# Attention with 32 heads beside a long convolution: one step of sixteen in four late stacks has its exponentials computed on VectorE, and the output projection is reordered

## The chip, the core and the metric

The kernel runs on one core of a Trainium2 chip. The core has five engines that run their own instruction streams and meet only through semaphores: TensorE (PE, matrix products, with its weight loads listed as PEld), VectorE (DVE), ScalarE (ACT, activation functions such as the exponential), GpSimd (POOL) and SyncE (SP, which here only issues DMAs). TensorE writes into PSUM, a small memory of eight banks; DVE and ACT read it from there. The metric is the device time of one execution in microseconds. The time before is 1044.47 us, the median of three runs (1041.78, 1044.47, 1046.85).

## What is computed

Two independent results stand side by side in the output, 2048 rows of 512 + 512 columns, all in float32.

```python
# A: attention, 32 heads of 16, one key and one value head for all of them
q = (x @ wq).reshape(B, S, H, Dh).transpose(0, 2, 1, 3)
k, v = x @ wk, x @ wv
p = softmax(einsum("bhqd,bkd->bhqk", q, k) * Dh ** -0.5)
a = einsum("bhqk,bkd->bhqd", p, v).transpose(0, 2, 1, 3).reshape(B, S, H * Dh) @ wo
...
# B: short causal convolution (4 taps) of k, times v, long causal convolution by FFT, gated by q
kv = shift_conv(k, shift_k) * v
y = irfft(rfft(pad(kv)) * rfft(pad(ssm_k))) + kv * ssm_D
b = q * y
```

Part A has 32 x 2048 x 2048 exponentials. They are the largest single piece of work in the kernel.

## The kernel before

**Attention.** The 32 heads times 2048 queries are cut into 32 *stacks* (`NQ`), each of four heads times 512 queries. A stack walks over the 2048 keys in 16 steps of 128 (`NKT`), and each step has two tiles of 128 keys by 2 x 512 scores. For each tile `scores` (the matmuls of L909) writes the scores into one of two PSUM buffers, `exp` (L921) has ACT turn them into probabilities in SBUF with one instruction of 128 x 1024, and `pv` (L941) multiplies both tiles of a step with V, extended by ones so that the row sums come along, into two PSUM banks that hold the sums of the whole stack. So there are 32 x 32 = 1024 exponential instructions. When a stack's last step is multiplied, DVE evicts the sums (L952, L953) and SP sends them to DRAM (L956). The last stack, 31, is cut in another way: two halves of 256 queries, each with 16 tiles.

**The frame.** `attend` is the main loop. One turn x is a *slot*: it emits the scores and the exponential of tile x + 2, then the V products that `plan` puts into this slot, and then hands the rest of the slot to `_Fill`. The order of every engine's instructions is thus written out when the program is built; nothing moves at run time, and an instruction that waits holds up all that follows it on its engine. The slot number within a stack is what is called "slot 14 of stack 26" below.

**The fill.** All other work runs as Python generators, called threads, which `_Fill.turn` asks in a fixed order, unless `hurry` puts one of them first. A thread asks for PE work as a number of units (216 ns each), with a charge for the DVE work that follows, or for DVE work alone (0 units and a charge in ns), or waits a number of steps of two slots (`WAIT`). PE units are given only as far as the account of the slot allows (916 ns a slot, 220 for scores, 430 for each half of a V product). DVE work is given while the credit is positive; it grows by 850 ns a slot, up to 1700. A thread whose next request is marked `CONT` holds the filler's PSUM pair, and no other thread gets PE work until it is done; after that two slots pass (`GAP`). The pool `pf` has two pairs of banks: one holds the sums of the running stack, the other is for the fill. Most fill matmuls go through `halves`: a first half, a tiny memset on DVE (`look`, L244) that marks its end, and a second half that waits for it. Their matmuls carry line L232.

**The threads**, in their order before: `wo_heads` brings the sums of two stacks (a *group* G of eight heads) back from DRAM, takes the reciprocal of the row sums (L1004, L1005), sends them through DRAM once more and forms normalised head outputs in 16-bit parts (L1016); `conv_pe` loads for the convolution and does its transforms on PE, in the order short transform of block 0, long transforms, output products of block 0 (`backward`, evicted by L450), short transform of block 1 (evicted by L272), output products of block 1; `conv_short` forms the short products on DVE; `rest_of_q` makes the other query chunks; `wo_part` does the output projection for chunks of 512 rows, each of four groups (L1058), then groups 12 and 13 (L1068), 14 (L1082), and the rest of the last group (L1095, after `over`, L1106 to L1112); `conv_dve` does the 16-point transforms and the products in the frequency domain on DVE (lines L152 to L203, L417); `spill` moves transposed inputs out to DRAM and back. Only four normalised groups fit at once, so group G waits until group G - 4 has been projected.

**The end.** After the last slot, `last` finishes the last V products, normalises the last quarter and adds its projection to the partial sums of the last chunk.

Of the kernel before, what the change touches and what calls it, by code (L numbers as in the profile page):

```python
# [8 lines left out]
F32 = mybir.dt.float32  # L9
F32R = mybir.dt.float32r  # L10
BF16 = mybir.dt.bfloat16
F16 = mybir.dt.float16
I32 = mybir.dt.int32
# [47 lines left out]
GAP = 2  # L61

# [36 lines left out]
class _Emit:  # L99
# [614 lines left out]
    def prologue(self):  # L714
        nc = self.nc
        zero = self.w.tile([P, 512], F16, tag="gn", bufs=3, name="zero")
        nc.vector.memset(zero, 0.0)
        self.load()
# [18 lines left out]
        nc.scalar.mul(self.wq[0][:, 0], self.wqf[0], WS)  # L737
        nc.vector.scalar_tensor_tensor(self.wq[0][:, 1], self.wqf[0], WS, self.wq[0][:, 0], ALU.mult, ALU.subtract)
# [11 lines left out]
        for g in range(1, 4):  # L750
            self.parts(nc.gpsimd, self.wq[g][:, 0], self.wq[g][:, 1], self.wqf[g], WS)
# [49 lines left out]
    def hurry(self):  # L801

        c, g = self.qn
        if c < 4 and self.step >= 2 * NKT * (4 * c + g) - LEAD:
            return 3
        return 4 if any(self.step >= x and ("wo", 4 * c) not in self.seen for c, x in enumerate(WO_AT)) else None
# [86 lines left out]
    def place(self, u):  # L893

        n = u // (2 * NKT)
        if n == NQ - 1:
            h = u // NKT % 2
            return n, u % NKT, slice(0, 2), slice(256 * h, 256 * h + 256)
        return n, u // 2 % NKT, u % 2, slice(0, 512)

    def scores(self, u):


        n, k, a, cols = self.place(u)
        s = self.ps.tile([P, 2, 512], F32, tag="s", name=self.nm("s"))
        for e in range(2):
            rows = slice(64 * e, 64 * e + KR)
            for j in range(0, P, 32):
                self.nc.tensor.matmul(  # L909
                    s[j : j + 32, e, :],  # L910
                    self.kst[rows, k * P + j : k * P + j + 32],
                    self.st[n][rows, a, cols],
                    start=True,
                    stop=True,
                )
        return s

    def exp(self, u, s):

        self.pt[u] = self.w.tile([P, 2, 512], F32, tag="p", bufs=PB, name=self.nm("p"))  # L920
        self.nc.scalar.activation(self.pt[u], s, AF.Exp, scale=DH**-0.5 / SC / SC)  # L921

    def pv(self, x, part):

        nc = self.nc
        n, k, _, cols = self.place(x)
# [4 lines left out]
        if k == 0:  # L931
            b = self.pair()
            self.acc = [b[:, 0, :], b[:, 1, :]]
        for e in range(2):
            rows = slice(64 * e, 64 * e + 64)
            for j in range(4):
                if wide:
# [3 lines left out]
                nc.tensor.matmul(  # L941
                    self.acc[e][32 * j : 32 * j + 32, m], self.vx[rows, k, :], y, start=k == 0, stop=k == NKT - 1
                )
        if k < NKT - 1:
            return
# [12 lines left out]
    def plan(self):  # L958


        plan = {}
        last = 2 * NKT * (NQ - 1)
        for x in range(0, last, 2):
            k = x // 2 % NKT
            if k == 1:
                for part, late in enumerate((1, 3)):
                    plan.setdefault(x + 1 + late, []).append((x, part))
            else:
                plan.setdefault(x + 1 + 2 * (k == 0), []).append((x, None))
        for x in range(last, 2 * NQ * NKT):  # L970
            plan.setdefault(x + {0: 2, 1: 1, 2: 1, 3: 1}.get(x % NKT, 0), []).append((x, None))
        cost = {i: sum(2 if x < last and part is None else 1 for x, part in v) for i, v in plan.items()}
        return plan, cost

    def attend(self, fill):
        self.od = self.dr.tile([NQ, P, 512], F32, name="od")
        tiles = 2 * NQ * NKT
        plan, cost = self.plan()
        for x in range(tiles - 2):
            t = x + 2  # L980
            if t % 32 == (22 if t < 32 else 12) and t // 32 + 1 < NQ:
                self.stack(t // 32 + 1)
            self.exp(t, self.scores(t))
            self.step, self.slot = x // 2, x
            for y in plan.get(x, []):
                self.pv(*y)
            fill.turn(x, cost.get(x, 0), cost.get(x + 1, 0))
# [3 lines left out]
    def heads(self, G):  # L991
# [10 lines left out]
        yield WAIT, 3  # L1002
# [10 lines left out]
        yield WAIT, 2  # L1013
# [35 lines left out]
    def wo_part(self):  # L1049
        nc, w, I = self.nc, self.w, self.I  # L1050
        xr = self.out.rearrange("b (c p i) d -> (b c) p i d", c=4, p=P, i=4)
        for c in range(3):
            yield from self.after(("oc", 4 * c + 3))
# [7 lines left out]
            self.seen.update(("wo", G) for G in range(4 * c, 4 * c + 4))  # L1061

# [8 lines left out]
        for q in range(2):  # L1071
            t = w.tile([P, D], F32, tag="xt", bufs=2, name=self.nm("wl"))
# [41 lines left out]
    def last(self, fill):  # L1114
# [5 lines left out]
        self.pv(2 * NQ * NKT - 2, None)  # L1120
# [4 lines left out]
        self.pv(2 * NQ * NKT - 1, None)  # L1125
# [14 lines left out]
class _Fill:  # L1140
# [29 lines left out]
    def give(self, t, n, i):  # L1170
        self.go(t, n or None)
        if n:
            self.holder = t if t[1] is not None and len(t[1]) > 2 and t[1][2] == CONT else None
            if self.holder is None:
                self.free = i + GAP

    def turn(self, i, pvs, more):
# [5 lines left out]
        while more:  # L1183
            more = False
            first = self.hurry()
            for t in sorted(self.threads, key=lambda t: t is not self.threads[first or 0]):
# [13 lines left out]
                self.give(t, n, i)  # L1200
# [131 lines left out]
def body(ctx, tc, I, out, parts="ab"):  # L1332
    fpool = ctx.enter_context(tc.tile_pool(name="fl", bufs=1))
    ok = fpool.tile([1, 1], I32, name="ok")
    with ExitStack() as st:
# [4 lines left out]
        threads = [em.wo_heads(), em.conv_pe(), em.conv_short(), em.rest_of_q(), em.wo_part(), em.conv_dve(), em.spill()]  # L1340
# [26 lines left out]
```

## Time and profile before

| | |
|---|---|
| median of three runs | 1044.47 us (1041.78 to 1046.85) |
| the profiled execution | 1042.55 us, its span 1040.5 us |
| mean granted TensorE clock | 0.979 of full speed |
| exponentials | 1024, 947.6 us of ACT's time |
| first and last exponential start | 32.55 us, 1021.2 us |
| from the last exponential's end to the end | about 18 us |
| DVE busy | 686.1 us of the span |

A row of the page gives busy time, share and number of instructions of each engine. The chain of work that ended last is followed back from the last instruction, at each step to what released it. Rows of instruction groups have the form: line, engine, operation, out<-in with shapes, count, then busy time, mean duration in ns, and the idle time of the engine before them with what ended it. Rows of a timeline have start, duration, engine, line, operation and count. "f" is the filler's PSUM pair (and the stack's sums), "s" a score tile, "p" its exponentials, "sp" a spectrum of the convolution, "ao" the evicted sums of a stack, "st" the queries of a stack, "xT" the transposed input.

### The profile page before, as it was taken

Reading aid. Unit: us, or ns where it says so; the run is one execution under the profiler, and the core shown is the slowest. Engines: PE = TensorE matmul, PEld = TensorE weight load, DVE = VectorE, ACT = ScalarE, POOL = GpSimd, SP = SyncE. Lnnn points to the kernel's source line nnn. Section 1 sums busy time; section 2 is a strip of 40 time slices with the busy share of each in tenths; the row PEclk is TensorE's granted clock in tenths of the full one; section 3 lists DMA queues with packets and bytes.
Section 4 is the critical chain, followed back from the end, with each engine's and each line's share of the span. In section 5 each row is a group of like instructions: output and inputs, shape, how many; then the busy total and the mean of one; then the engine's idle time right before and its main releaser. Section 6 shows DMA issues by size and latency. Waiting matters only on the chain.

```text
span 1040.5 us, 51057 instructions
## 1 busy us (share of the span) xinstructions
PE 956.9 (92%) x23391; PEld 466.4 (45%) x23391; DVE 686.1 (66%) x1023; ACT 960.1 (92%) x1040; POOL 171.2 (16%) x305
## 2 busy tenths in 40 slices
PE   7999999899988999999999999999988899999885
PEld 4344444344544444444444544544433344554352
DVE  4537866799626888989859843686898993221133
ACT  4599998899997999999999989999999999999983
POOL 2541304200031000010231423321000000330000
PEclk9699999999998999999999999999999999999998
DMA  6271524413252121211332324321111112330101
GB/s 228 84 213 50 163 86 106 105 48 89 63 103 72 44 70 39 75 45 53 87 108 78 106 87 125 109 75 51 48 49 47 36 41 63 105 124 20 52 3 44
DMA packets 69315, 83.11 MB, mean 80 GB/s; under 512 B 20800, under 2 KB 58278, under 8 KB 69094
## 3 DMA queue, kind: packets, MB, share of 16 engines
q1 hardware_dynamic: 47142, 43.51, 13.5%
q0 software_dynamic: 20320, 35.46, 12.2%
q8 instruction: 185, 3.03, 1.2%
q10 hardware_dynamic: 1632, 0.81, 0.3%
q14 instruction: 36, 0.29, 0.1%
HBM read 54.66 MB, written 25.03 MB: 77 GB/s over the span
## 4 chain that ended last, share of the span: by engine, by line
ACT 46%; PE 33%; issue 9%; DVE 8%; DMA 3%; SPq 0%; ACTq 0%; DVEq 0%
ACT p L921 46%; PE f L941 15%; PE s L909 9%; PE f L232 7%; DVE sp L152 2%; DMA rd<-rl 1%; DMA r<-rd 1%; DVE ao L952 1%; DVE ao L953 1%; DMA xb<-in_A_x 1%; PE f L600 1%; DVE sp L272 1%; DVE a L387 1%; DVE t L378 0%; DMA qd<-qp 0%
## 5 line engine op out<-in xcount | busy, mean ns | idle before, releaser
L921 ACT ACTIVATE p<-s 128x1024 f32<-128x1024 f32 x1024 | 947.6, 1067 | 42.3 <-PE s L909 39.5
L941 PE MATMUL f<-p,vx 64*32 64x512 f32 (+1 forms) x8944 | 561.4, 560 | 2.5 <-DVE sp L272 1.1
L909 PE MATMUL s<-st,kst 49*32 49x512 f16 x8192 | 431.3, 385 | 37.2 <-ACT p L921 33.9
L909 PEld LDWEIGHTS <-kst 49*32 49x32 f16 x8192 | 199.0, 90 | 404.3 <-issue 362.5
L941 PEld LDWEIGHTS f<-p,vx 64*32 64x32 f32 x8944 | 179.6, 107 | 37.2 <-issue 10.4
L152 DVE TENSOR_TENSOR sp<-sp 128x1024 f32<-128x1024 f32 x96 | 111.4, 1214 | 3.1 <-issue 1.9
L272 DVE COPY sp<-f 128x512 f32<-128x512 f32 x64 | 41.1, 684 | 51.2 <-PE f L232 50.9
L277 POOL DMA_DIRECT2D ff<-in_ff x64 | 34.3, 545 | 199.8 <-PE s L909 192.3
L152 DVE TENSOR_TENSOR sp<-sp,sp 128x1024 f32<-128x1024 f32 x48 | 56.0, 1216 | 5.2 <-issue 3.6
L232 PE MATMUL f<-wo,o 64*32 64x512 f16 x1440 | 56.6, 375 | 3.0 <-DVE look L244 3.0
L452 POOL DMA_DIRECT2D out<-r x32 | 17.5, 550 | 247.6 <-DVE r L450 247.6
L244 DVE MEMSET look<- 128x4 f32 x67 | 4.2, 62 | 80.5 <-PE f L232 80.5
L232 PE MATMUL f<-xT,wq 64*32 64x512 f16 x1344 | 51.6, 376 | 5.1 <-DVE gm L712 2.6
L232 PE MATMUL f<-hT,ff 64*32 64x256 f32 x1024 | 42.8, 385 | 9.2 <-DVE look L244 8.5
L952 DVE COPY ao<-f 128x512 f32<-128x512 f32 (+1 forms) x33 | 22.3, 675 | 38.3 <-PE f L941 38.2
L232 PE MATMUL f<-a,ff 64*32 64x256 f32 x1024 | 42.0, 378 | 4.3 <-DVE look L244 3.4
L232 PE MATMUL f<-sp,fi 64*32 64x256 f32 x1024 | 41.0, 383 | 1.8 <-DVE look L244 1.8
L369 POOL DMA_DIRECT2D v<-in_B_v x32 | 17.0, 536 | 121.9 <-PE s L909 55.0
L378 DVE TENSOR_TENSOR t<-kk,tpb 128x512 f32<-128x512 f32 (+1 forms) x50 | 33.0, 663 | 3.1 <-issue 2.7
L387 DVE TENSOR_TENSOR a<-a,t 128x512 f32<-128x512 f32 x48 | 33.2, 691 | 2.6 <-DVE t L378 1.2
L450 DVE TENSOR_TENSOR r<-f,q 128x256 f32<-128x256 f32 x32 | 12.1, 419 | 32.0 <-PE f L232 32.0
L232 PEld LDWEIGHTS <-o 64*32 64x32 f16 x1440 | 22.8, 93 | 16.3 <-DVE look L244 3.6
(154 smaller groups left out, 681.6 us busy)
## 6 DMA issues: line engine op xcount, KB each, us to landing
ff<-in_ff POOLq DMA_DIRECT2D x64, 128.0 KB, 3.3
od<-ao SPq DMA_DIRECT2D x60, 128.0 KB
qd<-qp SPq DMA_DIRECT2D x48, 128.0 KB
st<-qd SPq DMA_DIRECT2D x62, 98.0 KB
kk<-in_B_k POOLq DMA_DIRECT2D x32, 128.0 KB, 3.9
v<-in_B_v POOLq DMA_DIRECT2D x32, 128.0 KB, 2.6
hin<-in_B_ssm_k POOLq DMA_DIRECT2D x32, 128.0 KB, 6.9
fi<-in_fi POOLq DMA_DIRECT2D x32, 128.0 KB, 3.5
```

The costliest lines, as they stand in the source:

```text
L152: v.tensor_tensor(part(out), part(a), part(b), op)
L232: y = self.nc.tensor.matmul(out[j : j + 32, cols], w[r, j : j + 32], x[r], start=half == m == 0, stop=half == 1 and m == k - 1,)
L272: self.nc.vector.tensor_copy(c[:, :, m + i, :], b[i].rearrange("p (q n) -> p q n", q=2))
L277: self.nc.gpsimd.dma_start(t[:, i], self.I[n][:, 2 * m2 + i])
L369: nc.gpsimd.dma_start(v[:, i], self.vr[:, 2 * m2 + i, cs])
L378: nc.vector.tensor_tensor(out[:, n], kk[:, x], tap(i, n.stop - n.start), ALU.mult)
L387: nc.vector.tensor_tensor(a, a, t, ALU.add)
L452: nc.gpsimd.dma_start(self.orr[:, 2 * m2 + i, D + blk * CB : D + (blk + 1) * CB], r[:, i])
L909: self.nc.tensor.matmul(s[j : j + 32, e, :], self.kst[rows, k * P + j : k * P + j + 32], self.st[n][rows, a, cols], start=True, stop=True,)
L921: self.nc.scalar.activation(self.pt[u], s, AF.Exp, scale=DH**-0.5 / SC / SC)
L941: nc.tensor.matmul(self.acc[e][32 * j : 32 * j + 32, m], self.vx[rows, k, :], y, start=k == 0, stop=k == NKT - 1)
L952: nc.vector.tensor_copy(a, self.acc[0][:, m])
```

## The change

In stacks 27, 28, 29 and 30 the last step, keys 1920 to 2047, is taken out of the main loop: `tiles` lists the tiles that remain, 30 instead of 32 in these stacks, and 1016 in all. A new thread `own`, first in the order, computes this step. It takes a pair of the filler's PSUM for the scores of each of the two tiles, from slot 14 of the stack before. On DVE it then adds a large constant that rounds the score to a whole number (the scores now come in units of ln 2, since the query weights are divided by it), subtracts again to get the fraction, builds the power of two by writing the rounded part as a 16-bit integer whose bits are read as a bfloat16 exponent, and evaluates a polynomial of the fraction by five fused multiply-add passes, the last of which multiplies by the power of two. The probabilities come out scaled by a constant, which a scaled copy of V (`vo`) takes back. From slot 8 of the stack, `attend` adds the product of this step in two parts.

```diff
+OWN_IN = (27, 28, 29, 30)
+OWN_AT, OWN_PV = 14, 8
...
-        self.nc.scalar.activation(self.pt[u], s, AF.Exp, scale=DH**-0.5 / SC / SC)
+        self.nc.scalar.activation(self.pt[u], s, AF.Exp, scale=LN2 * DH**-0.5 / SC / SC)
...
+    def own(self):
...
+        for n in OWN_IN:
+            while self.slot < 32 * n - 32 + OWN_AT or self.owed:
+                yield WAIT, 1
+            for a in range(2):
+                yield (1, 2400, CONT, 1, 4) if a else (1, 2400, NEW, 1)
+                b = self.pair()
+                self.keys(b, n, OWN, a, slice(0, 512))
+                v.tensor_scalar(self.po[:, a], b, MAGIC, None, ALU.add)
+                v.scalar_tensor_tensor(f[:, a], self.po[:, a], MAGIC, b, ALU.subtract, ALU.subtract)
+                if a == 0:
+                    yield WAIT, 1.5, CONT
+            for a in range(2):
+                g, y = self.po[:, a], f[:, a]
+                x = self.w.tile([P, 2, 512], I16, tag="s2", bufs=S2, name=self.nm("x"))
+                yield 0, 900
+                v.tensor_scalar(x, g, 2.0**-11, (127 - DOWN) * 128 - MAGIC * 2.0**-11, ALU.mult, ALU.add)
+                for i in range(4, -1, -1):
+                    yield 0, 1220
+                    v.scalar_tensor_tensor(g, g if i < 4 else y, c[i], y if i else x.bitcast(BF16), ALU.add, ALU.mult)
+            self.owed = [(-1 - n, part) for part in range(2)]
...
-            if t % 32 == (22 if t < 32 else 12) and t // 32 + 1 < NQ:
-                self.stack(t // 32 + 1)
+            n = self.at[t][0]
+            if t - self.base[n] == (6 if n else 22) and n + 1 < NQ:
+                self.stack(n + 1)
...
+            if self.owed and self.owed[0][0] == -1 - n:
+                part, in_stack = self.owed[0][1], x - self.base[n]
+                if in_stack >= 5 + part * (NKT - 1) if n == NQ - 1 else in_stack >= OWN_PV and not pvs:
+                    pvs = [self.owed.pop(0)] + pvs
```

The output projection changes its order: chunk 1 also waits until block 1's short transform is done, and chunk 2 is done in two pieces, groups 8 to 10 into a partial sum in SBUF, then group 11 on top of it. The pauses in the head work get shorter, and the two zero-padded weight tiles of the last group (`wl`) lie in another buffer, since `own` uses theirs (`xt`).

```diff
-        yield WAIT, 3
+        yield WAIT, 2
         yield 0, 400
         nc.vector.tensor_scalar(l, l, 1e-30, 1 / OS, ALU.max, ALU.mult)
...
-        yield WAIT, 2
+        yield WAIT, 1.5
...
-        for c in range(3):
-            yield from self.after(("oc", 4 * c + 3))
+        for c in range(2):
+            yield from self.after(("oc", 4 * c + 3), *[("cx", 1)] * c)
...
+        yield from self.after(("oc", 10), "q3")
+        wp = [w.tile([P, D], F32, tag="wq", bufs=4, name=self.nm("wp")) for _ in range(4)]
+        for i in (0, 2):
+            b = yield from self.wo_rows(i, range(8, 11), 1400)
+            for r in range(2):
+                nc.vector.tensor_scalar(wp[i + r], b[r], 1 / (OS * WS), None, ALU.mult)
+        self.seen.update(("wo", G) for G in range(8, 11))
+        yield from self.after(("oc", 11))
+        for i in (0, 2):
+            b = yield from self.wo_rows(i, [11], 1400)
+            for r in range(2):
+                t = self.s2("wp", (512,))
+                nc.vector.scalar_tensor_tensor(t, b[r], 1 / (OS * WS), wp[i + r], ALU.mult, ALU.add)
...
-            t = w.tile([P, D], F32, tag="xt", bufs=2, name=self.nm("wl"))
+            t = self.s2("wl", (512,))
...
-        threads = [em.wo_heads(), em.conv_pe(), em.conv_short(), em.rest_of_q(), em.wo_part(), em.conv_dve(), em.spill()]
+        threads = [em.own(), em.wo_heads(), em.conv_pe(), em.conv_short(), em.rest_of_q(), em.wo_part(), em.conv_dve(), em.spill()]
```

More of the change, by code (lines that the diff above doesn't have):

```diff
@@ L968, in plan @@
             else:
[L969 to L972, printed above, removed]
-        return plan, cost
+                plan.setdefault(x + 1 + 2 * (k == 0), []).append((x, None, x + 2 == self.base[n + 1]))
+        for x in range(last, len(self.at)):
+            k = self.at[x][1]
+            plan.setdefault(x + {0: 2, 1: 1, 2: 1, 3: 1}.get(k, 0), []).append((x, None, k == self.at[-1][1]))
@@ new lines, in plan @@
+        cost = {i: sum(2 if x[0] < last and x[1] is None else 1 for x in v) for i, v in plan.items()}
+        return plan, cost
+    def own(self):
+        nc, v = self.nc, self.nc.vector
+        c = [x / TWO[5] * (-(2.0**18)) ** (5 - i) for i, x in enumerate(TWO)]
+        self.vo = self.msk[:, 163:195]
+        done = [f"q{c}" for c in range(4)]
+        yield from self.after(*done)
+        yield 0, 100
+        v.tensor_scalar(self.vo, self.vx[:, OWN, :], -TWO[5] * 2.0 ** (DOWN - 90), None, ALU.mult)
+        room = [self.w.tile([P, 2, 4, 512], F16, tag="xt", bufs=2, name=self.nm("own")) for _ in range(2)]
+        self.po = room[0].rearrange("p i k n -> p (i k n)").bitcast(F32).rearrange("p (a e n) -> p a e n", a=2, e=2)
+        f = room[1].rearrange("p i k n -> p (i k n)").bitcast(F32).rearrange("p (a e n) -> p a e n", a=2, e=2)
+        for n in OWN_IN:
[18 more added lines that the diff above has]
+            self.owed = [(-1 - n, part) for part in range(2)]
+        self.seen.add("own")
```

84 lines of the change are left out of this document (53 added, 31 removed).

## The prediction, made before the changed kernel was run

> **What bounds the kernel now.** First the page: span, busy shares and the chain of work that ended last.
>
> ```profile
> span 1040.5 us, 51057 instructions
> PE 956.9 (92%) x23391; PEld 466.4 (45%) x23391; DVE 686.1 (66%) x1023; ACT 960.1 (92%) x1040; POOL 171.2 (16%) x305
> ACT 46%; PE 33%; issue 9%; DVE 8%; DMA 3%; SPq 0%; ACTq 0%; DVEq 0%
> ```
>
> ACT and PE are equally busy over the span, so the answer has to come from the stage that changes. Next, the timeline of ACT alone at the end (start, duration, line, operation, count; idle before it in brackets), then a table by stretches of one stack each, 26 to 30, and last stack 31 (length, then busy time of PE, weight loads, DVE, ACT, POOL; granted clock).
>
> ```profile
> 839.25 162.56 ACT L921 ACTIVATE p<-s 128x1024 f32<-128x1024 f32 x177
> 1004.45 1.02 ACT L921 ACTIVATE p<-s 128x1024 f32<-128x1024 f32 x1 [2.64 <-PE s L909]
> 840.98:870.30 29.32, 28.64 (x760) 13.88 (x752) 24.32 (x30) 29.32 (x33) 0.00 (x0) 1.00 0.12 37
> 870.30:899.63 29.33, 27.97 (x728) 14.15 (x720) 6.92 (x16) 29.33 (x33) 6.41 (x12) 1.00 0.35 110
> 899.63:928.96 29.33, 29.20 (x776) 15.17 (x768) 7.18 (x19) 29.33 (x33) 10.69 (x20) 1.00 0.41 128
> 928.96:958.29 29.33, 28.73 (x760) 14.13 (x752) 4.22 (x10) 29.33 (x33) 3.14 (x6) 1.00 0.12 38
> 958.29:987.62 29.33, 25.66 (x624) 11.70 (x616) 5.40 (x11) 29.33 (x33) 0.00 (x0) 1.00 0.17 47
> 987.62:1022.30 34.68, 31.14 (x984) 19.84 (x968) 11.28 (x28) 31.06 (x34) 0.00 (x0) 0.95 0.02 4
> 872.93 0.69 DVE L952 COPY ao<-f 128x512 f32<-128x512 f32 x1
> 902.32 0.69 DVE L952 COPY ao<-f 128x512 f32<-128x512 f32 x1 [0.43 <-PE f L941]
> ```
>
> From 839 to 1002 there is no idle moment between 177 exponentials: 162.56/177 = 0.918 us each. A stack is 32 of them, 29.3 us, and the eviction that closes a stack (L952) comes 902.32 - 872.93 = 29.39 us after the one before. ACT sets the pace in stacks 27 to 30, while DVE works only 4 to 7 of each 29.3 us there (24 of 29.3 in stack 26). So an exponential taken away in this stage is worth its full 0.918 us, as long as neither PE nor DVE takes over.
>
> **The change, part by part.** *Eight exponentials go.* Stacks 27 to 30 lose both tiles of step 15, two exponentials each: 8 x 0.918 = -7.3 us. Their score matmuls and their products with V stay on PE, moved into the fill between the steps. The rescaling of the query projection by 1/ln 2 alters constants of existing instructions and costs nothing.
>
> *What DVE gets.* Per tile: two passes out of PSUM (rounding, fraction), one to 16-bit integers, five fused passes for the polynomial. DVE's groups with shapes kept apart (busy, mean ns of one):
>
> ```profile
> L201 DVE TENSOR_SCALAR u<-sp 128x1024 f32<-128x1024 f32 x18 | 12.4, 689 | 0.4
> L575 DVE SCALAR_TENSOR_TENSOR xT<-f,xT 128x1024 f16<-128x1024 f32 x4 | 4.8, 1220 | 3.3 <-ACT xT L572 3.3
> L152 DVE TENSOR_TENSOR sp<-sp 128x1024 f32<-128x1024 f32 x96 | 111.4, 1214 | 3.1 <-issue 1.9 <-DVE sp L152 1.2
> L1058 DVE TENSOR_SCALAR wp<-f 128x512 f32<-128x512 f32 x12 | 7.7, 686 | 24.2 <-PE f L232 24.2
> ```
>
> A one-tensor pass from PSUM has a row only at half width, 0.69; full width lies between that and twice it, and I take 1.22, like the fused pass from PSUM. The integer pass is nearest to L201, 0.69 (at most 1.22). A fused pass in SBUF with two full tensors is nearest to L152, 1.22. One tile: 2 x 1.22 + 0.69 + 5 x 1.22 = 9.2 us; a stack 18.5, all four 74 us. The chain of stack n starts at slot 14 of stack n-1; it charges the filler 2 x 2400 + 2 x (900 + 5 x 1220) = 18800 ns, which at 850 ns per slot takes 22 slots, so it ends at slot 4 to 6 of stack n, before slot 8 where its product may enter. The idle DVE time of the stretches (29.3 - 7.2 = 22 us at the least) covers 18.5 us: 0 on the path. Without that cover it would cost 74 us.
>
> The Trainium skill's page ScalarE: Activation LUTs, section Rules for kernel authors, speaks against the change: exp belongs on ScalarE, as the only option. As a price the rows agree with it, 9.2 us on DVE against 0.918 on ACT, and by that rule the sum would be 8 x 9.2 - 7.3 = +66 us if DVE were on the path; the stretches show that it is not, so this gets no chance of its own.
>
> *PSUM for the moved scores.* The filler has two pairs of banks, one of them held by the stack's sums, so the second score tile waits until DVE has read the first twice: 2 x 1.22 = 2.4 us plus the hand-over, say 3.1, against three slots of 0.918 = 2.75. PE has per slot 0.916 - 0.22 - 0.43 = 0.27 us to spare by the kernel's own figures, and no other fill runs while the tile is held, 0.8 us in three slots, which covers the 0.35: 0. If a whole pass of DVE is ahead of it, 1.22 - 0.45 = 0.8 us each: 0 to +3.2 us for four.
>
> *Stack ends under a busy DVE.* In the middle of the run DVE and fill are both busy, and ACT idles about once a stack, at its end. Of nine such rows in eleven stack ends the first, the largest, the smallest and the last, and then the same place in a late stack, in all engines' timeline:
>
> ```profile
> 418.10 28.90 ACT L921 ACTIVATE p<-s 128x1024 f32<-128x1024 f32 x31 [1.81 <-PE s L909]
> ...
> 603.00 30.46 ACT L921 ACTIVATE p<-s 128x1024 f32<-128x1024 f32 x33 [2.86 <-PE s L909]
> 634.33 58.93 ACT L921 ACTIVATE p<-s 128x1024 f32<-128x1024 f32 x63 [0.87 <-PE s L909]
> ...
> 727.66 1.03 ACT L921 ACTIVATE p<-s 128x1024 f32<-128x1024 f32 x1 [2.02 <-PE s L909]
> 903.04 0.69 DVE L953 TENSOR_TENSOR ao<-ao,f 128x512 f32<-128x512 f32 x1
> 903.76 0.06 DVE L244 MEMSET look<- 128x4 f32 x1
> 903.90 0.64 PE L232 MATMUL f<-sp,fi 64*32 64x256 f32 x16
> ```
>
> At 903.04 DVE runs the two evictions, then the small memset that lets the second half of a fill group start, and PE starts it 0.08 us after that: no slack even with an idle DVE. Behind a polynomial pass (up to 1.22 us) PE waits. The middle's rows range from 0.87 to 2.86 us. The polynomial of the next stack is under way at all four ends (26/27 to 29/30). I take the lowest row, 0.87, at two of the four, since a fill group stands at that point only part of the time: +1.7 us; bounds 0 and 4 x 2.86 = +11.4, which would make the sum +4.1.
>
> *Projection order.* Chunk 1's projection now waits for the second block's short transform, chunk 2's is split into 8..10 early and 11 alone. PE, then the end of that transform on DVE, the start and the end of DVE's long transform:
>
> ```profile
> 624.74 0.63 PE L232 MATMUL f<-wo,o 64*32 64x512 f16 x16
> ...
> 648.08 0.67 PE L232 MATMUL f<-a,ff 64*32 64x256 f32 x16
> 713.89 1.29 DVE L272 COPY sp<-f 128x512 f32<-128x512 f32 x2 [3.51 <-PE f L232]
> 715.10 6.89 DVE L152 TENSOR_TENSOR sp<-sp 128x1024 f32<-128x1024 f32 x6
> 843.61 0.69 DVE L952 COPY ao<-f 128x512 f32<-128x512 f32 x1
> ...
> 861.97 4.63 DVE L152 TENSOR_TENSOR sp<-sp,sp 128x1024 f32<-128x1024 f32 x4
> ```
>
> Chunk 1's first half held PE from 624.7 to 648; without it the short transform starts up to 23 us earlier, and DVE's transform with it. It ends at 866.6 now; 20 us earlier, plus four extra evictions (4 x 0.69) and some 5 us of evictions and head work drawn forward into it, gives about 854. Slot 14 of stack 26 is at about 856 (stack 25 closes at 843.6; 14 x 0.918 = 12.9 on). So the inverse transform is just out of the way, the block's output products start earlier than now, and they still end in time although the four score pairs hold the filler some 9 slots each. Value 0; stalls like those above shift within stacks 20 to 24, -3 to +3.
>
> *Small moves.* The two loads of the next stack's queries are issued 6 slots earlier, ahead of the head loads in SP's queue; 8 slots (7.3 us) remain until the moved scores need them: 0. The zeroed weights move to another buffer whose last users are done: 0. Shorter pauses in the head work issue its DVE steps 2 and 1 slots earlier; where DVE then waits for a DMA, everything behind it waits too (the rival below): 0 here, because in stacks 28 to 30 I expect little fill at those moments. The tail after 1022.3 stays.
>
> Sum: -7.3 + 1.7 = -5.6 us. The profiled execution took 1042.55 us (span 1040.5 and 2.05 around it), so 1036.95 in its terms; the median of the three runs is 1.92 higher, 1044.47, and I forecast 1044.47 - 5.6 = 1038.9.
>
> **Rivals.** *PE becomes the bound* (chance 0.18). PE's score group in 870 to 988:
>
> ```profile
> L909 PE MATMUL s<-st,kst 49*32 49x512 f16 x1032 | 53.1, 381 | 5.7 <-ACT p L921 5.4
> ```
>
> PE waited for ACT only 5.4 us in four stacks. If all its work stays there, no more than 5.4 can be won: -5.4 + 1.7 = -3.7, 1040.8. Against it: chunk 2's second half and the start of the output products leave this window for the earlier one.
>
> *Contention takes most* (0.17). If all four ends stall, by about the mean of the four rows shown, (1.81 + 2.86 + 0.87 + 2.02)/4 = 1.9 us, two of them at the cost of the smallest, that is 2 x 1.9 + 2 x 0.87 = 5.5: -7.3 + 5.5 = -1.8, 1042.7. For it speaks the missing slack at 903.9, against it that DVE then does only the polynomial and a few evictions, and not two threads at once as in the middle.
>
> *Slower: DVE blocked behind a DMA* (0.12). Head 14, in stack 30:
>
> ```profile
> 969.99 0.18 DVE L1004 TENSOR_SCALAR rl<-rl 128x32 f32<-128x32 f32 x1 [5.94 <-DMA rl<-od]
> 977.73 0.69 DVE L1016 TENSOR_TENSOR o<-of,r 128x512 f16<-128x512 f32 x1 [7.17 <-DMA r<-rd]
> ```
>
> DVE's queue stood 5.94 and 7.17 us for these loads, and it hurts nobody now since no fill group runs then. The pauses before them shrink, so it stands longer. If the output products or projection 12, 13 slip into stack 30, their memset is queued behind, PE stops, and ACT with it: 13.1 us less about 1 us that PE has in hand each time, 11: -7.3 + 1.7 + 11 = +5.4, 1049.9. It decides if DVE's inverse transform is still running at 856: the polynomial has priority, takes the next 22 slots, and pushes the output products back by 20 us. That ACT and DVE queues are strict FIFO is stated by the Trainium skill, TensorE: Matmul & The Clock Gate, section Architectural detail; a stall that long is what this rule would give here.
>
> The change could also not do what it says, if the products of the moved step waited for the polynomial at slot 8; that shows as a PE wait and is inside the contention rival.
>
> **How the numbers follow.** Forecast 0.50, its own range 1037.2 to 1041 (no stall at an end, -7.3, to four short ones, -7.3 + 3.5 = -3.8); PE bound 0.18; contention 0.17; slower 0.12; 0.03 for a larger gain, if the last stack's 2.64 us stall at 1004 also goes. The range 1034 to 1048.6 ends above where the bound of the stack ends would put it (+4.1), so it leaves out the slower case; it begins 2.64 us and a little below the forecast's own range, for that stall. About 0.5% (5.2 us) is what a measurement of this kernel can tell from no change. Faster by more than that needs two stalls or fewer at the four ends, at even odds for each 11 cases in 16 of the forecast, 0.34; with a third of the PE case, 0.06, and the larger gain, 0.03, it is 0.44 rounded up. Slower by more is the slower case, 0.12, and the rest, 0.44, lies within.
>
> **What would show it.** 1016 exponentials, the late ones at 0.918 us; four DVE blocks of some 18.5 us from slot 14 on; stack ends 30 slots (27.5 us) apart in stacks 27 to 30; ACT idle below 1 us at those ends. Wrong if a fused pass takes clearly more than 1.22 us, if the output products run into stack 30, or if PE waits for the polynomial or for DVE's PSUM reads by more than a microsecond per stack.

## The result, and the profile after

The changed kernel takes 1054.8 us (median of twelve runs, 1048.4 to 1059.92) and the kernel before, run beside it, 1041.68 us (twelve runs, 1037.94 to 1046.95). The ratio is 1.0112, 95% interval 1.0082 to 1.0142. It is 1.1% slower; 1038.9 us was forecast, and the time lies above the range (1034 to 1048.6). The profiled execution of the changed kernel is its slowest, 1059.92 us, so its differences to the profile of before (17.6 us in span) are somewhat larger than those of the medians (13.1 us).

The page's span, its busy times, and the chain of work that ended last:

```profile
span 1058.1 us, 51250 instructions
PE 960.1 (91%) x23455; PEld 469.8 (44%) x23455; DVE 760.1 (72%) x1094; ACT 955.2 (90%) x1032; POOL 171.3 (16%) x305
PE 36%; ACT 35%; issue 12%; DVE 11%; DMA 3%; POOL 2%; SPq 0%; ACTq 0%; POOLq 0%; DVEq 0%
```

ACT lost eight instructions and DVE gained 74.0 us of work; the polynomial's own instructions (L1016, L1017, L1024, L1027) are 73.4 of them, where 74 was priced. But ACT's share of the chain fell from 46 to 35%, and PE, DVE and issue took it over. Now ACT's timeline at the place where it ran 162 us without an idle moment before:

```profile
839.52 44.17 ACT L940 ACTIVATE p<-s 128x1024 f32<-128x1024 f32 x48
886.07 1.02 ACT L940 ACTIVATE p<-s 128x1024 f32<-128x1024 f32 x1 [2.39 <-PE s L928]
887.94 26.74 ACT L940 ACTIVATE p<-s 128x1024 f32<-128x1024 f32 x29 [0.84 <-PE s L928]
917.39 27.80 ACT L940 ACTIVATE p<-s 128x1024 f32<-128x1024 f32 x30 [2.70 <-PE s L928]
948.30 1.02 ACT L940 ACTIVATE p<-s 128x1024 f32<-128x1024 f32 x1 [3.11 <-PE s L928]
950.43 1.02 ACT L940 ACTIVATE p<-s 128x1024 f32<-128x1024 f32 x1 [1.11 <-PE s L928]
...
981.85 1.03 ACT L940 ACTIVATE p<-s 128x1024 f32<-128x1024 f32 x1 [3.75 <-PE s L928]
983.62 25.82 ACT L940 ACTIVATE p<-s 128x1024 f32<-128x1024 f32 x28 [0.74 <-PE s L928]
```

44.17/48 is still 0.920 us for one exponential. Each stack now has a stall of 2.4 to 3.75 us a few exponentials after it begins, three of the four with a smaller one behind. The table by waits (who waits for what, in all, times, longest) for 878.9 to 1005.6, stacks 27 to 30, says what stands behind them:

```profile
ACT p L940 <- PE s L928: 15.3, 9, 3.8
PE f L243 <- DVE look L255: 11.1, 4, 3.1
```

The same table of before has neither of these two rows for stacks 27 to 30. ACT waits for scores, because PE waited, four times, once at each end of a stack, for the tiny memset `look` on DVE. Here is the end of stack 26, DVE, PE and ACT:

```profile
881.27 0.69 DVE L974 TENSOR_TENSOR ao<-ao,f 128x512 f32<-128x512 f32 x1
...
881.88 1.22 DVE L1027 SCALAR_TENSOR_TENSOR own<-own 128x1024 f32<-128x1024 f32 x1
...
883.13 1.23 DVE L1027 SCALAR_TENSOR_TENSOR own<-own,own 128x1024 f32<-128x1024 f32 x1
884.30 0.06 DVE L255 MEMSET look<- 128x4 f32 x1
...
884.44 1.11 PE L243 MATMUL f<-sp,fi 64*32 64x256 f32 x16 [2.12 <-DVE look L255]
...
885.29 0.68 PE L928 MATMUL s<-st,kst 49*32 49x512 f16 x8
...
885.71 1.88 PE L964 MATMUL f<-p,vx 64*32 64x512 f32 x16
886.07 1.02 ACT L940 ACTIVATE p<-s 128x1024 f32<-128x1024 f32 x1 [2.39 <-PE s L928]
```

DVE evicts the sums of the stack (L973, L974), then runs two polynomial passes, and only then the memset of 0.06 us. PE stands 2.12 us in front of the second half of a fill group, and the scores for ACT are queued behind it. It is the place that the prediction showed at 903.76, one stack earlier and with 2.4 us of passes pushed in front. Then PE runs slowly: the scores take 0.68 and the V product 1.88 us, 0.41 and 1.05 a few steps later; at three of the four ends that brings ACT a second stall. By stretches of one stack (26 to 30; length, busy time of PE, weight loads, DVE, ACT, POOL, granted clock):

```profile
849.60:878.90 29.30, 26.78 (x672) 12.94 (x672) 13.89 (x18) 29.30 (x33) 3.20 (x6) 1.00 0.22 65
878.90:909.90 31.00, 28.16 (x688) 13.49 (x673) 16.69 (x24) 27.77 (x31) 9.61 (x18) 0.94 0.31 94
909.90:940.40 30.50, 26.40 (x672) 13.46 (x672) 22.55 (x29) 27.74 (x31) 4.28 (x8) 1.00 0.22 71
940.40:973.40 33.00, 29.05 (x672) 13.88 (x672) 21.99 (x26) 28.08 (x32) 3.14 (x6) 0.90 0.10 33
973.40:1005.60 32.20, 28.87 (x728) 13.38 (x735) 20.49 (x26) 27.71 (x32) 0.00 (x0) 0.95 0.15 43
```

The four stacks take 31.0, 30.5, 32.9 and 32.2 us, 126.6 together, where 4 x 27.5 = 110 was meant and 117.5 was before. And 180 us into the run stands a stall that has nothing to do with the moved steps; DVE, PE and ACT:

```profile
177.23 0.06 DVE L255 MEMSET look<- 128x4 f32 x1 [2.63 <-PE f L243]
188.17 0.69 DVE L1082 TENSOR_TENSOR o<-of,r 128x512 f16<-128x512 f32 x1 [10.88 <-DMA r<-rd]
...
191.57 0.61 PE L701 MATMUL f<-qa,wb 128*32 128x512 bf16 x1 [9.49 <-DVE sp L283]
192.87 1.02 ACT L940 ACTIVATE p<-s 128x1024 f32<-128x1024 f32 x1 [9.36 <-PE s L928]
```

Head group 1 has DVE multiply by the reciprocals of its row sums before they are back from DRAM; DVE stands 10.88 us, the eviction behind it (L283) comes late, PE waits 9.49 us for that and ACT 9.36 us. Stack 4 takes 43.7 us (35.1 before), stack 5 29.6 (31.5).

### The profile page after: what moved, and what is told of

Read it like the earlier page. It is cut to its first block, busy times and chain, and to the rows that moved or that the text cites. A ratio compares the mean times of both kernels' runs of the same rounds, so it can differ in the third digit from the quotient of the medians.

```text
span 1058.1 us, 51250 instructions
## 1 busy us (share of the span) xinstructions
PE 960.1 (91%) x23455; PEld 469.8 (44%) x23455; DVE 760.1 (72%) x1094; ACT 955.2 (90%) x1032; POOL 171.3 (16%) x305
## 3 DMA queue, kind: packets, MB, share of 16 engines
q1 hardware_dynamic: 47142, 43.51, 13.1%
## 4 chain that ended last, share of the span: by engine, by line
PE 36%; ACT 35%; issue 12%; DVE 11%; DMA 3%; POOL 2%; SPq 0%; ACTq 0%; POOLq 0%; DVEq 0%
ACT p L940 35%; PE f L964 16%; PE s L928 9%; PE f L243 8%; DVE sp L163 1%; DVE own L1027 1%; DVE ao L973 1%; DVE ao L974 1%; DVE sp L283 1%; DMA r<-rd 1%; DVE a L398 1%; POOL out L463 1%; DMA rd<-rl 1%; DMA xb<-in_A_x 1%; DVE t L389 1%
## 5 line engine op out<-in xcount | busy, mean ns | idle before, releaser
L283 DVE COPY sp<-f 128x512 f32<-128x512 f32 x64 | 41.2, 685 | 42.4 <-PE f L243 42.0
L288 POOL DMA_DIRECT2D ff<-in_ff x64 | 34.3, 542 | 214.5 <-PE s L928 196.6
L243 PE MATMUL f<-sp,fi 64*32 64x256 f32 x1024 | 41.8, 387 | 9.8 <-DVE look L255 9.8
L973 DVE COPY ao<-f 128x512 f32<-128x512 f32 (+1 forms) x33 | 22.2, 673 | 29.5 <-PE f L964 29.4
L398 DVE TENSOR_TENSOR a<-a,t 128x512 f32<-128x512 f32 x48 | 33.1, 690 | 11.9 <-issue 10.2
L461 DVE TENSOR_TENSOR r<-f,q 128x256 f32<-128x256 f32 x32 | 12.1, 419 | 33.7 <-PE f L243 33.6
L243 PEld LDWEIGHTS f<-hT,ff 64*32 64x32 f32 x1024 | 20.9, 107 | 21.4 <-issue 9.1
```

What stands on the lines that cost most here:

```text
L243: y = self.nc.tensor.matmul(out[j : j + 32, cols], w[r, j : j + 32], x[r], start=half == m == 0, stop=half == 1 and m == k - 1,)
L283: self.nc.vector.tensor_copy(c[:, :, m + i, :], b[i].rearrange("p (q n) -> p q n", q=2))
L288: self.nc.gpsimd.dma_start(t[:, i], self.I[n][:, 2 * m2 + i])
L398: nc.vector.tensor_tensor(a, a, t, ALU.add)
L973: nc.vector.tensor_copy(a, self.acc[0][:, m])
```

## The experiments

Lengths of stacks below run from the first exponential of one stack to that of the next, counted in each kernel's trace, which is one execution; the medians are of 4 to 12 executions. Each ratio is to the kernel before, run beside it (median 1040.82 us beside e1 to e4, 1039.04 beside e5 to e7, 1040.85 beside e8 and e9, 1042.54 beside e10 and e11).

| run | median us | ratio (95%) | stacks 27 to 30, us | stack 4 |
|---|---|---|---|---|
| before | 1041.68 | | 29.4, 29.3, 29.5, 29.3 | 35.1 |
| after | 1054.8 | 1.0112 (1.0082 to 1.0142) | 31.0, 30.5, 32.9, 32.2 | 43.7 |
| e1 no moved steps | 1039.98 | 0.9989 (0.9962 to 1.0015) | 29.4, 29.3, 29.5, 29.3 | 43.0 |
| e2 and old pauses | 1042.5 | 1.0008 (0.9982 to 1.0034) | 29.4, 30.1, 29.4, 29.3 | 34.8 |
| e3 one fused pass | 1052.95 | 1.0116 (1.0065 to 1.0167) | 27.6, 30.1, 33.1, 31.7 | 44.9 |
| e4 ends charged 1400 | 1043.43 | 1.0019 (0.999 to 1.0047) | 28.3, 29.2, 27.8, 29.4 | 44.9 |
| e5 two passes alone | 1053.98 | 1.0111 (1.006 to 1.0162) | 31.4, 32.9, 33.5, 29.3 | 42.3 |
| e6 ends charged 2600 | 1038.35 | 0.9987 (0.9962 to 1.0012) | 27.6, 27.5, 27.6, 27.8 | 44.9 |
| e7 passes pause | 1041.77 | 1.0002 (0.9972 to 1.0032) | 27.7, 27.5, 28.8, 27.7 | 41.8 |
| e8 e6, head 1 as before | 1031.68 | 0.9902 (0.9867 to 0.9938) | 27.6, 27.5, 27.6, 27.8 | 35.2 |
| e9 and head 8 as before | 1031.81 | 0.991 (0.9879 to 0.9942) | 27.6, 27.5, 27.6, 27.8 | 39.6 |
| e10 e8, no moved steps | 1034.85 | 0.994 (0.9914 to 0.9967) | 29.4, 29.3, 29.5, 29.3 | 35.1 |
| e11 e8 again | 1033.75 | 0.992 (0.9896 to 0.9943) | 27.6, 27.5, 27.6, 27.8 | 34.0 |

### Which part of the change loses: e1, e2

```diff
-OWN_IN = (27, 28, 29, 30)
+OWN_IN = ()
```

> The changed kernel without its moved steps: no stack gives up a step, all 1024 exponentials on ACT; projection order, pauses and early loads of the change stay. Theory A (the polynomial passes queue in front of the small memset at stack ends, 16.5 us in the profiled run against 7.3 saved): the late stacks come back to 29.3 us each, and the time falls by about 9 from 1054.8, to 1044 to 1047; what is left above 1041.7 belongs to order and pauses. Rival B (order and pauses alone make it slower): the late stacks were never the cause, and the time stays at 1053 or above.

Without the moved steps the kernel is as fast as before, below what theory A gave. So the new order and the shorter pauses cost nothing net, and the whole loss hangs on the moved steps.

e2 is e1 with the pauses of the head work as before (3 and 2):

```diff
-        yield WAIT, 2
+        yield WAIT, 3
         yield 0, 400
...
-        yield WAIT, 1.5
+        yield WAIT, 2
         for out, a, b, op
```

> As the run before, and the pauses in the head work are again 3 and 2 steps: only projection order, early query loads and the buffer of the zeroed weights are left of the change. If the shorter pauses block DVE behind the load of the reciprocals in every run (9.4 us of idle ACT in stack 4 of the profiled run, 8.5 us more than before), this is 6 to 9 us faster than the run with the short pauses, about 1038 to 1041. If that stall was an accident of one execution, the two are within 2 us.

A miss: e2 isn't 6 to 9 us faster than e1, but 2.5 us slower. Stack 4 did get its 8 us back, but stack 5 takes 34.6 instead of 29.6 and stack 31 (to the end of its last exponential) 33.5 instead of 30.6. From the first exponential of stack 0 to that of stack 27 e1 takes 847.2 us and e2 839.8. The short pauses lose 7 us early and win 9 us from stack 27 to the end, 5.3 of them behind the last exponential.

### The length of the chain or its place: e3

Four of the five fused passes are left out, so DVE does 2 x 4 x 1.22 = 9.8 us less per stack.

```diff
-                for i in range(4, -1, -1):
+                for i in (0,):
                     yield 0, 1220
```

> The changed kernel with one of the five fused passes of each polynomial left (four are left out, so the probabilities of these steps are not exponentials). Moved scores, PSUM reads, products and order are all as in the change; DVE's chain shrinks from 18.5 to about 8.7 us a stack and ends before the stack does. Theory A: stack ends no longer stall, late stacks take 27.5 to 28 us, 1054.8 - 14 = about 1041, 1039 to 1044. Rival C (the moved scores' hold on the filler's PSUM pair or PE's load is the cause): late stacks stay at 30 us or more, 1052 or above.

A miss that told most: half of the chain is gone and nothing is won. The end of stack 26 in this run's timeline, DVE:

```profile
878.57 0.69 DVE L974 TENSOR_TENSOR ao<-ao,f 128x512 f32<-128x512 f32 x1
...
879.28 0.06 DVE L255 MEMSET look<- 128x4 f32 x1
```

And the end of stack 27, DVE and PE:

```profile
907.09 0.69 DVE L974 TENSOR_TENSOR ao<-ao,f 128x512 f32<-128x512 f32 x1
907.69 0.68 DVE L1024 TENSOR_SCALAR x<-own 128x1024 int16<-128x1024 f32 x1
...
908.41 1.23 DVE L1027 SCALAR_TENSOR_TENSOR own<-own,x 128x1024 f32<-128x1024 f32 x1
...
909.59 0.06 DVE L255 MEMSET look<- 128x4 f32 x1
...
909.71 0.67 PE L243 MATMUL f<-sp,fi 64*32 64x256 f32 x16 [2.54 <-DVE look L255]
```

At the first end no pass stands between eviction and memset, and stack 27 takes 27.6 us, the full gain. At the second two passes do, and PE waits 2.54 us. At the two ends after that two or three passes stand there again. What counts is not how long the chain is, but whether a piece of it stands in front of the memset in the few slots around a stack's end.

### Two passes by themselves, and one fewer at the ends: e5, e4

e5 is e1 (`OWN_IN = ()`) with two meaningless passes of the same size behind the evictions of stacks 26 to 30, on a scratch buffer (zeroed once by POOL) whose content nothing uses. No exponential is taken from ACT.

```diff
                 nc.sync.dma_start(self.od[n, :, i : i + CB], a[:, i : i + CB])
...
+        if 26 <= n < 31:
+            z = self.po[:, 0]
+            for _ in range(2):
+                nc.vector.scalar_tensor_tensor(z, z, 1.0, z, ALU.add, ALU.mult)
```

> No moved steps (all exponentials on ACT, as in the first run), but behind the two evictions that close stacks 26 to 30 DVE does two fused passes of 128x1024 on a scratch tile, 2.4 us each time. Theory A' (what counts is how many passes stand between the evictions and a memset that follows at once, not how long the chain is): ACT stalls only at the ends of stacks 26 and 30, where the memset follows the evictions within 0.1 us in the run without moved steps, by 2 to 3 us each, and not at the three other ends, where the next memset comes 7 us or more later: 4 to 6 us over 1039.98, 1044 to 1046. Rival (any DVE work at a stack's end costs): all five ends stall, 10 us or more. Rival (the passes are innocent, the moved scores are not): no stall, 1040.

Five pairs of passes, 5 x 2.48 = 12.4 us of DVE work on an engine that is busy for 29 of the 128.5 us there, make the kernel 1.1% slower, as much as the whole change. Stalls appear at four ends instead of the expected two, so theory A' was too narrow, and the result is nearer to the first rival (any DVE work at a stack's end costs). At the end of stack 27 there is no `look` to wait for; DVE and PE of e5 there:

```profile
914.19 2.48 DVE L983 SCALAR_TENSOR_TENSOR own<-own 128x1024 f32<-128x1024 f32 x2
...
916.59 0.74 DVE L461 TENSOR_TENSOR r<-f,q 128x256 f32<-128x256 f32 x2
...
917.38 1.79 PE L964 MATMUL f<-p,vx 64*32 64x512 f32 x16 [1.83 <-DVE r L461]
```

The first V product of the new stack needs the PSUM pair that the fill has just used, and the eviction that frees it (L461) stands behind the passes. So a stack's end has two hand-overs through DVE; only the end of stack 29, where the fill pauses, is free of cost, so it isn't the work itself that costs but a hand-over behind it.

e4 takes 1400 ns from the filler's credit at each late end, so that it grants fewer passes there:

```diff
                 self.pv(*y)
+                if y[2:] == (True,) and n >= 26:
+                    fill.credit -= 1400
```

> The changed kernel, with the two evictions at a stack's end from stack 26 on charged to the filler's DVE account (1400 ns), so that at least one polynomial pass is issued later, behind the memset and not ahead of it. Theory A with a backlog: PE's wait for the memset falls from about 3.0 to 1.8 us or less, the time by 4 to 7 us to 1048 to 1051. If the passes ahead of the memset do not depend on this account, no change (within 2 us of 1054.8).

The direction is right and the gain larger than expected (1043.43, below the 1048 to 1051). At most one fused pass is left in front of each memset instead of two, and ACT's stalls at the four ends are 0.47, 1.44, 0 and 1.64 us.

### No pass in front of the hand-over: e6, e7

e6 is e4 with 2600 instead of 1400.

> The changed kernel with 2600 ns instead of 1400 charged to the filler's DVE account at each stack's end from stack 26 on. Theory A': no fused pass is left between evictions and memset, ACT's waits at the four stack ends fall below 0.5 us each, the four stacks take 27.5 to 28.2 us each (the run with 1400: 28.3, 29.2, 27.8, 29.4), and the time is 3 to 4 us below that run's 1043.4: 1039 to 1041. If the ends still stall by over 1 us with no pass ahead of the memset, theory A' falls.

Right, with the time 0.65 us below the range. The end of stack 26 in e6, DVE and PE's weight loads:

```profile
880.86 0.69 DVE L974 TENSOR_TENSOR ao<-ao,f 128x512 f32<-128x512 f32 x1
...
881.69 1.22 DVE L1027 SCALAR_TENSOR_TENSOR own<-own 128x1024 f32<-128x1024 f32 x1
881.71 0.06 DVE L255 MEMSET look<- 128x4 f32 x1
881.83 0.19 PEld L243 LDWEIGHTS f<-sp,fi 64*32 64x32 f32 x16 [0.22 <-DVE look L255]
```

And ACT's timeline of e6 from stack 26 on:

```profile
835.50 157.29 ACT L940 ACTIVATE p<-s 128x1024 f32<-128x1024 f32 x171
993.31 9.49 ACT L940 ACTIVATE p<-s 128x1024 f32<-128x1024 f32 x10 [0.52 <-PE s L928]
1005.19 16.66 ACT L940 ACTIVATE p<-s 128x1024 f32<-128x1024 f32 x18 [2.39 <-PE s L928]
```

The memset now stands beside the first pass instead of behind two; 157.29/171 = 0.920, no idle moment, and the four stacks take 110.4 us together. The same 74 us of polynomial work costs nothing there.

e7 reaches this in another way: none of the five fused passes is issued from slot 26 of a stack to slot 2 of the next.

```diff
                 for i in range(4, -1, -1):
+                    while self.slot % 32 >= 26 or self.slot % 32 < 3:
+                        yield WAIT, 0.5
                     yield 0, 1220
```

> The changed kernel, with the polynomial's passes not issued from slot 26 of a stack to slot 2 of the next. Theory A': as with the larger charge, no pass stands before the memset; four stacks of 27.5 to 28.2 us, 1038 to 1042. If the products of the moved steps, which come later now, push the output products back into stack 31, the last stack is longer than 34.3 us instead.

Right, but for the end of stack 28, where ACT stalls 0.97 us: two passes of the head work (L1084, 0.69 us each) stand between evictions and memset there, and PE waits 1.35 us. The last stack takes 34.7 us, a little more than the 34.3 that was named as the other outcome. Two edits with nothing in common but the place of the passes both win the loss back, and e5 makes the same loss with passes alone, which settles it.

### The stall of head group 1: e8, e9

```diff
-        yield WAIT, 2
+        yield WAIT, 3 if G in (1,) else 2
         yield 0, 400
...
-        yield WAIT, 1.5
+        yield WAIT, 2 if G in (1,) else 1.5
```

> The run with 2600 ns charged, and in the head work of group 1 alone the old pauses of 3 and 2 steps. If the shorter pauses make DVE stand 10.9 us for the reciprocals of group 1 and ACT stall in stack 4 in every run (44.9 us against 35.1 before in that run's profile), stack 4 comes back to 35 to 38 us, and the time falls by 4 to 8 us to 1031 to 1035, clear of the kernel before. If the stall only moves on (the run with all old pauses lost 3.2 us in stack 5), 1035 to 1038.

Right: e6 with the old pauses in this one group is faster than both kernels. In e9 group 8 has them as well (`G in (1, 8)`), to see whether it causes the stall of stack 18 (36.8 us in e6, 32.4 before):

> As the run before, with the old pauses for group 8 too, whose head work falls in stack 18 (36.8 us in the run with 2600 ns charged, 31.4 with all old pauses). If the pauses of group 8 cause that stall, stack 18 falls to 31 to 33 us and the time by another 3 to 5 us, to 1028 to 1032. If it is the load of the transform's table that PE waits for there (3.3 us in the changed kernel) whatever the pauses, no change against the run before.

Stack 18 doesn't change (36.9): PE still waits 3.3 us there for a load of the transforms' table (`ff`). So it isn't group 8, although the median lies in the range that was given for it. Why that load is late stays open; in e2, with all the old pauses, the same stack takes 31.4. The profiled execution of e9, its slowest of eight (1041.15 us), also shows that the old pauses shorten the stall of group 1 and don't end it: DVE still stands 5.49 us for the reciprocals there (2.87 in e8), and stack 4 takes 39.6 us.

### What the moved steps are worth once they stall nothing: e10, e11

e6 is no faster than e1, though its four stacks are 7.2 us shorter. e10 is e8 with `OWN_IN = ()` and without the charge, e11 is e8 once more, run beside it.

> Head group 1 has its old pauses, and no step is moved (OWN_IN is empty): e8 without the moved steps and without the doubled charge. It asks what the moved steps are worth once they stall nothing. In e6 four late stacks were 7.2 us shorter than in e1 (110.4 against 117.6 us), but its span was the same, 1040.1 against 1040.3: the last stack was 2.5 us longer and the tail after the last exponential 4.1 us longer (18.3 against 14.2). Theory A, the fill sets the end, so the time taken from ACT comes back in the last stack and the tail: as fast as e8 within about 2 us, 1030 to 1034. Theory B, e6 and e1 were equal by accident of where the early fill went, and the moved steps are worth their 7 us: 1037 to 1041, with e8 7 us ahead of it in this call.

> The kernel of e8 once more, to stand beside e10 on the same chip: moved steps, charge of 2600 at the late stack ends, old pauses for head group 1. By theory A of e10 both take 1030 to 1034; by theory B this one takes 1030 to 1034 and e10 1037 to 1041. By both the stacks 27 to 30 are 27.5 us long, and the tail behind the last exponential is 18 us or more here and shorter in e10.

Theory B falls, and theory A holds but for e10's median 0.85 us above its range: the two medians lie 1.1 us apart, less than the half width of either interval (0.24 to 0.27%, 2.4 to 2.8 us), so a gain of that size stays open, but not one of 7. Of the 7.2 us (117.6 and 110.4 us for the four stacks) the profiles keep nothing. In e11 the last stack takes 34.3 us instead of 30.6, and the time from the last exponential's end to the span's end is 19.7 us instead of 14.0. The last rows of the fill on DVE, and what PE does with them, show where they go. DVE in e10:

```profile
1008.18 1.28 DVE L1178 TENSOR_TENSOR wp<-wp,f 128x512 f32<-128x512 f32 x2 [5.79 <-PE f L243]
...
1011.11 0.42 DVE L1195 TENSOR_TENSOR lr<-ao,lr 128x256 f32<-128x256 f32 x1
```

PE in e10, the first product of the final projection:

```profile
1014.72 1.07 PE L225 MATMUL x<-wl,lr 128*32 128x512 f32 x8
```

DVE in e11, the same two steps:

```profile
1010.88 1.28 DVE L1180 TENSOR_TENSOR wp<-wp,f 128x512 f32<-128x512 f32 x2 [3.63 <-PE f L243]
...
1013.81 0.42 DVE L1197 TENSOR_TENSOR lr<-ao,lr 128x256 f32<-128x256 f32 x1
```

And PE in e11, the same product:

```profile
1014.44 1.94 PE L225 MATMUL x<-wl,lr 128*32 128x512 f32 x8 [2.46 <-issue]
```

Both start the final projection at the same moment, 1014.7 and 1014.4. In e10 the normalised part (L1195) has been ready for 3 us and PE comes from the last V products. In e11 PE is done with them earlier and stands idle 2.46 us until L1197 is ready. The same wait stands some 21 us earlier, in the middle of e11's last stack: PE waits 2.19 us for the first normalised parts, and ACT, behind it, 2.33 and 1.11 us. After the second wait PE is slow: the granted clock from 1014.4 to the end is 0.70 in e11 and 0.87 in e10, and e11 takes 17.5 us from there, e10 14.2.

So in e11 the fill comes last, not ACT: output products, projection and normalisation, one behind the other. It takes part of every slot, so fewer slots, with score and V products moved into it, don't end it sooner; the convolution's last output product starts at 950.0 us in e11 and at 909.0 in e10. That the moved products are what delays it is read from these times; no run tests it by itself. The kernel before already ends in this way, DVE and PE:

```profile
1023.93 0.43 DVE L1112 TENSOR_TENSOR lr<-ao,lr 128x256 f32<-128x256 f32 x1
...
1024.56 1.07 PE L214 MATMUL x<-wl,lr 128*32 128x512 f32 x8 [2.45 <-issue]
```

Its last exponential ends at 1022.3, and PE waits until the normalised part is there at 1024.36.

## Why the prediction was wrong

**Held.** An exponential costs 0.918 us; the passes cost what was read from the nearest rows (1.22 for the passes from PSUM and the fused ones, 0.69 to integers, 73.4 us in all). "PSUM for the moved scores, 0" held: with the ends cleared (e6) ACT has no idle moment in those stacks. "Projection order, 0" held over the run (e2, 1.0008, which has the order without the pauses). The inverse transform on DVE was done in time, even before stack 26 began (847.9 us against 849.6).

**The step that failed: "Stack ends under a busy DVE", +1.7 us.** The mechanism was named, with the row that shows it; the size was off tenfold. The term took the smallest stall of the middle, 0.87, at two ends of four. Measured: all four ends stall, ACT stands 15.3 us in the four stacks, and they take 16.2 us more than in e6 without the stalls. Even the bound, 4 x 2.86 = 11.4, was too low. Three things were missed. Two passes stand in front of the memset, not a part of one, because the filler grants them back to back at that moment. Nearly always something stands there that needs DVE within a slot or two: a fill group's second half, or the new stack's first V product, as e5 shows (four ends of five). And PE runs slower after three of these four waits, which costs a second stall. The prediction's own sign of being wrong, PE waiting for the polynomial by more than a microsecond per stack, is what came: 11.1 us in four stacks.

**A second step failed, unseen in the total: -7.3 for the exponentials.** It was to hold "as long as neither PE nor DVE takes over". In stacks 27 to 30 it held once the ends were cleared (e6, e11); the last stack and the tail take it back, 3.7 and 5.8 us in e11 against e10. What failed is the step from an exponential in these stacks to the end of the run: the fill comes last there, and it comes last in the kernel before as well. "The tail stays" was right against before (18.3 and 18.2 us); the new order with the shorter pauses brings it to 14 us (e1, e10; 19.4 with the old pauses, e2), and the moved steps undo that.

**"Small moves, 0" held only as a sum.** The shorter pauses cost 7 us in front of stack 27 and win it back from there on (e1 against e2). The prediction looked for a DVE that stands for a DMA in stack 30 and found it harmless; it stood in stack 4.

**The rivals.** "Contention takes most" was the right mechanism, priced at 5.5 us. The argument brought against it, that DVE does only the polynomial there and not two threads, was the error: one thread with a credit puts its passes just as well in front of the memset. "PE becomes the bound" was wrong in its stretch (e6 runs 27.5 us a stack); it was right only in that something other than ACT sets the end of the run. "Slower: DVE blocked behind a DMA" had the sign and not the place: DVE waits 0.70 us for that load in stack 30 (999.39 us).

## What to carry to other kernels

An engine that idles half of the time isn't free: ask which small instruction on it another engine waits for, and at which moments, and keep long passes away from there; here 12.4 us of idle-time work cost 1.1%. Work taken from the engine that sets the pace pays only if what ends last shortens too, so follow the chain to the end of the run before counting it. And look at a neutral sum for two large terms of opposite sign: putting one group's pauses back won 0.5% (e1 to e10) to 0.9% (e6 to e8), which no part of the change itself did.

## What was not expected of the hardware

After a wait of 2 to 3 us PE mostly comes back slow. The ends of stacks 27 and 28 in the changed kernel, PE's first instruction after the wait and the V product behind it:

```profile
916.40 0.67 PE L243 MATMUL f<-sp,fi 64*32 64x256 f32 x16 [3.08 <-DVE look L255]
...
917.08 1.07 PE L964 MATMUL f<-p,vx 64*32 64x512 f32 x16
...
946.66 1.11 PE L243 MATMUL f<-sp,fi 64*32 64x256 f32 x16 [2.84 <-DVE look L255]
...
947.94 1.96 PE L964 MATMUL f<-p,vx 64*32 64x512 f32 x16
```

The wait of 2.12 us at the end of stack 26 (shown above) is followed by a product of 1.88 us, that of 3.08 us by one at nearly full speed: the length of the wait alone doesn't decide it. Over the 3 us behind these two waits the granted clock is 0.50 and 1.00; behind the one of 2.84 us it is 0.53 over 6 us. In the whole trace it changes only on one fixed grid of 3.41 us. The waits of 2.12 and 2.84 us leave PE busy for 0.51 and 0.53 of one window of that grid, and the clock is 0.5 in the next; the wait of 3.08 us is split over two windows, busy for 0.57 and 0.50, and nothing follows. With shares so near to each other these rows don't give the threshold. The Trainium skill, TensorE: Matmul & The Clock Gate, section What's actually happening, has the clock fall after an idle window of about 3.4 us, in windows that run freely. The grid, which doesn't start with the wait, agrees with that; a window that is idle throughout doesn't, since PE was busy for half of each.

The way of head group 1's reciprocals (128 x 32 numbers) to DRAM and back: DVE has them at 170.9 us after the change and can use them at 188.2, 17.3 us later. In e8 they are ready 5 us later, at 176.0, and can be used at the same moment, 188.15. So something else than the reciprocal sets it. Of the two hops, the one to DRAM takes 7.3 us after the change and 8.3 in e8 (from its issue on SP to that of the way back), the one back 9.9 and 3.9. In both runs thirteen to fifteen loads of the convolution's filter, 128 KB each, land between 173 and 189 us; whether the reciprocals wait behind them was not tried.
